# RWKV attention fused with an MLP: four chunks in pairs instead of six, other PSUM banks for the first pair, and weights loaded behind the second pair

## The chip, the cores and the metric

The kernel runs on one core of a Trainium2 chip. The core has five engines with an instruction stream each: TensorE (PE, matmuls and transposes into PSUM; PEld is its weight load), VectorE (DVE), ScalarE (ACT), GpSimd (POOL) and SyncE (SP, which issues transfers here). Sixteen DMA engines move data between HBM and the on-chip buffer SBUF. Each engine executes its own stream in order; semaphores make one wait for another. The metric is the device time of one execution in microseconds (us), lower is better.

## What is computed

Two steps in a row. The first is a recurrence with a decaying state per batch (4) and head (8), over 768 positions with 48 channels; the second is a two-layer MLP on the 3072 x 384 result.

```python
for t in range(S):                      # S = 768, B = 4, H = 8, D = 48
    cur = einsum('bhd,bhe->bhde', u[None] * k_t, v_t)
    y[:, :, t] = einsum('bhd,bhde->bhe', r_t, state + cur)
    state = w_t[..., None] * state + einsum('bhd,bhe->bhde', k_t, v_t)
x = y.transpose(0, 2, 1, 3).reshape(B * S, H * D)   # 3072 x 384
h = x @ w_in                            # 384 x 2048
g = maximum(0.01 * h, h)
out = g @ w_out                         # 2048 x 384
```

The decays w lie between 0.8 and 0.95. All inputs and the output are float32; the kernel multiplies in bfloat16 and accumulates in float32.

## The kernel before

The 3072 positions are 24 **chunks** of 128, six a batch. Inside a chunk the recurrence is made of matmuls: the logarithm of w (ScalarE) is summed along positions by a matmul with a triangular matrix of -1 (`cp`), its exponentials scale r and k (`rk`, products on VectorE), both are transposed (`rkT`, four 128 x 128 transposes for each of r and k, evacuated by VectorE from the bank `se` and by ScalarE from `so`), `scores` multiplies them, VectorE masks the result (`m`), and `intra` adds masked scores times v (`vb`) and scaled r times the incoming state (`sb`). The term with u is not in the matmuls: GpSimd multiplies r by u (`ru`) and by k, VectorE sums over channels (`dg`), GpSimd multiplies by v (`vs`), and VectorE adds that to the PSUM result (`y`). `outer` gives the new state. y is transposed into `xT`; then 4 groups of 12 up-projection matmuls a chunk (`hp`, leaky ReLU on ScalarE into `g`) and 4 quarters of 4 down-projection matmuls (`op`) make the output.

Some chunks come in **pairs**: 256 positions, of which every SBUF row holds two neighbours (j = 0, 1), so that a load has contiguous rows of 384 bytes instead of 192. A pair's matmuls work on two 64-row halves (`ab`, `par`, `q`).

The order of all engines is fixed when the program is built. `Plan` holds every step with an engine, an assumed duration, dependencies and a priority, and a list scheduler replays them; the instructions are then issued in the order found. A changed duration or priority in the source therefore changes orders, not work.

```python
    OACT = 14
    NCI = 3        # direct sums by matmul only for chunks below this
    NPE = 14       # from chunk 14 on, transposes go by DMA
    LEAD = 4       # logarithm of chunk n waits for the first up-projection of n - LEAD
    AHEAD = 5
    PAIRS = (0, 2, 4)
    WEIGHTS = [(2, 4.0)] * 2 + [(4, 24.0)] * 4 + [(6, 44.0)] * 2   # (chunk, priority)
    CASTS = 2
...
    hp_r = ring("hp", 2, [128, 512], F32, psum)
    op_r = ring("op", 2, [128, DM], F32, psum)
    cp_r = ring("cp", 1, [128, 512], F32, psum)
    yp_r = pp_r = ring("yp", 1, [128, 512], F32, psum)
    se_r = ring("se", 1, [128, NP, 128], F32, psum)
    so_r = ring("so", 1, [128, NP, 128], F32, psum)
```

Of a pair, the outer products, the state and the products with it:

```python
            for ab in range(2):
                q0 = 64 * ab
                ...                                      # sb: the incoming state, scaled on GpSimd
                pp = yp_r.take()
                def outer(pp=pp, q0=q0):
                    for p in range(NP):
                        for j in range(2):
                            nc.tensor.matmul(
                                pp.t[:, p * 2 * D : (p + 1) * 2 * D],
                                lhsT=rk[j].t[q0 : q0 + 64, 1, 2 * p : 2 * p + 2, :].rearrange("p h d -> p (h d)"),
                                rhs=vb[j].t[q0 : q0 + 64, 2 * p : 2 * p + 2, :].rearrange("p a d -> p (a d)"),
                                start=(j == 0), stop=(j == 1), skip_group_check=True)
                ...
            for jt in range(2):
                sc = [se_r.take(), so_r.take()]
                ...                                      # 32 score matmuls, mask
                def intra(m=m, yp=yp, jt=jt):
                    for ab in range(2):
                        if sbs[ab] is None: continue
                        for p in range(NP):
                            q = 64 * ab
                            nc.tensor.matmul(yp.t[q : q + 64, 2 * p * D : (2 * p + 2) * D],
                                lhsT=rkT[jt].t[:, p, q : q + 64], rhs=sbs[ab]..., ...)
                    ...                                  # 32 products of masked scores with v
```

Each of the eight weight loads (768 KB of w_in or w_out) is followed by a cast to bfloat16, half on VectorE and half on ScalarE. The row u is loaded by SyncE and spread over 128 partitions by a float32 matmul with a column of ones (`op` bank), then copied by ScalarE.

Of the kernel before, what the change touches and what calls it, by code (L numbers as in the profile page):

```python
# [15 lines left out]
class Plan:  # L16
# [5 lines left out]
    def __init__(self):  # L22
        self.eng, self.dur, self.fn, self.deps, self.pri, self.wire = [], [], [], [], [], []

    def add(self, eng, dur, fn, deps, pri, wire=None):

        i = len(self.eng)
        self.eng.append(eng)
        self.dur.append(dur)
        self.fn.append(fn)  # L30
        self.deps.append(sorted({d for d in deps if d is not None}))
        self.pri.append(pri)
        self.wire.append(wire)
        return i

    def order(self):
# [11 lines left out]
        dma_free = 0.0  # L48
        for i in range(n):
            if not left[i]:  # L50
                heapq.heappush(coming[self.eng[i]], (0.0, i))
# [3 lines left out]
        while events:  # L55
# [13 lines left out]
            free[e] = now + self.dur[i] * (1.8 if e == "PE" and now < 18 else 1)  # L69
            if self.wire[i] is None:  # L70
                done[i] = free[e] + self.LAT[e]
            else:
                dma_free = max(dma_free, free[e]) + self.wire[i]
                done[i] = dma_free + 1.6
            heapq.heappush(events, (free[e], e))
            for j in users[i]:
                left[j] -= 1
                ready_at[j] = max(ready_at[j], done[i])
# [37 lines left out]
def kernel(  # L116
# [26 lines left out]
    LEAD = 4  # L143
    AHEAD = 5

    PAIRS = (0, 2, 4)
    PWIRE, WIRE = 1.3, 1.15
    WEIGHTS = [(2, 4.0)] * 2 + [(4, 24.0)] * 4 + [(6, 44.0)] * 2
    CASTS = 2
# [43 lines left out]
    g_r = ring("g", 4, [128, NJ, max(blocks) * L], BF16)  # L193
# [3 lines left out]
    op_r = ring("op", 2, [128, DM], F32, psum)  # L197
    cp_r = ring("cp", 1, [128, 512], F32, psum)
    yp_r = pp_r = ring("yp", 1, [128, 512], F32, psum)
    se_r = ring("se", 1, [128, NP, 128], F32, psum)  # L200
    so_r = ring("so", 1, [128, NP, 128], F32, psum)

    with tc.manual_schedule():
# [51 lines left out]
        def step(eng, dur, fn, pri, reads=(), writes=(), deps=(), wire=None):  # L255
# [4 lines left out]
            i = plan.add(eng, dur, fn, d, pri, wire)  # L260
# [16 lines left out]
        def weight_steps(q, which, pri):  # L277
# [14 lines left out]
            ld = step("SP", 0.45, load, pri, writes=[st], wire=2.0)  # L292
# [44 lines left out]
        def product(rk, a, xn, e, P0, deps, n):  # L337
            return step(
                "DVE", 0.6 if n < 4 else 0.84 - 0.04 * a,
# [25 lines left out]
        def turn(rk, rkT, s_d, n, P0):  # L365

            if n >= NPE:
# [4 lines left out]
                    P0, reads=[rk], writes=[rkT], deps=s_d, wire=1.6)]  # L372
            made = []
            for a, eng in ((0, "DVE"), (1, "ACT")):
                tr = (se_r, so_r)[a].take()
                trv = tr.t[:].bitcast(BF16).rearrange("p g t -> p (g t)").rearrange("p (g t) -> p g t", t=128)
# [20 lines left out]
        def masked(m, sc, mask, s_sc, P0):  # L397
# [4 lines left out]
                        out=m.t[:, par], in0=sc[par].t[:],  # L402
# [14 lines left out]
        def state(sx, pp, sb, P0, deps):  # L417

            def f():
                i = pp.t[:, 0:DM].rearrange("p (g a d) -> p g a d", g=NP, a=2)  # L420
# [8 lines left out]
        def finish(yp, vs, s_y, s_vs, n, P0):  # L429
# [7 lines left out]
            if n >= NPE:  # L437
# [4 lines left out]
                    P0 + 1, reads=[y], deps=[s_ye], wire=0.65))  # L442
# [15 lines left out]
        def load_in(use, src, P0, i, n, wire, view):  # L458
            return step(
                "SP", 0.45, lambda: nc.sync.dma_start(out=view(use), in_=src), P0 + 0.1 * i,  # L460
                writes=[use], wire=wire, deps=[cums[n - AHEAD]] if n >= AHEAD else [])

        def spread_u():
            u_row = step(
                "SP", 0.45,
                lambda: nc.sync.dma_start(out=ur[:], in_=u.rearrange("h d -> (h d)").unsqueeze(0)),
                0.15, wire=0.05)
# [3 lines left out]
                lambda: nc.tensor.matmul(up.t[:], lhsT=onef[:], rhs=ur[:], start=True, stop=True),  # L471
                0, writes=[up], deps=[u_row])
            return step(
                "ACT", 0.5, lambda: nc.scalar.copy(out=ub[:], in_=up.t[:]), 3, reads=[up], deps=[s_ub])
# [6 lines left out]
        def pair(n):  # L481
# [89 lines left out]
            for j in range(2):  # L571
                s_T += turn(rk[j], rkT[j], s_d[j], n, P0)
# [3 lines left out]

            sbs, s_sbs = [], []
            for ab in range(2):
                q0 = 64 * ab
# [10 lines left out]
                pp = yp_r.take()  # L590

                def outer(pp=pp, q0=q0):
                    for p in range(NP):
                        for j in range(2):
                            nc.tensor.matmul(  # L595
                                pp.t[:, p * 2 * D : (p + 1) * 2 * D],
                                lhsT=rk[j].t[q0 : q0 + 64, 1, 2 * p : 2 * p + 2, :].rearrange("p h d -> p (h d)"),
                                rhs=vb[j].t[q0 : q0 + 64, 2 * p : 2 * p + 2, :].rearrange("p a d -> p (a d)"),
                                start=(j == 0), stop=(j == 1), skip_group_check=True)

                s_pp = step(
                    "PE", 0.35, outer, P0 + 1, reads=[*rk, *vb], writes=[pp],
                    deps=[s_d[0][1], s_d[1][1], *s_vb])
                sx = sx_r.take()
                prev = (sx, [state(sx, pp, sb, P0, [s_pp, *s_sb])])

            for jt in range(2):

                sc = [se_r.take(), so_r.take()]

                def scores(sc=sc, jt=jt):
                    for p in range(NP):
                        for js in range(2):
                            for q in (0, 64):
                                for par in range(2):
                                    q0 = 64 * par
                                    nc.tensor.matmul(
                                        sc[par].t[q : q + 64, p, 64 * js : 64 * js + 64],
# [4 lines left out]
                s_sc = step("PE", 0.6, scores, P0 + 1, reads=rkT, writes=sc, deps=s_T)  # L623
# [4 lines left out]
                def intra(m=m, yp=yp, jt=jt):  # L628
                    for ab in range(2):
                        if sbs[ab] is None:  # L630
                            continue
                        for p in range(NP):
# [18 lines left out]
                    "PE", 0.8, intra, P0 + 1, reads=[m, *vb, rkT[jt], *there], writes=[yp],  # L651
# [267 lines left out]
```

## Time and profile before

| | before |
|---|---|
| median of 3 runs | 196.09 us (195.69 to 196.6) |
| profiled span | 195.8 us |
| TensorE busy | 180.3 us (92%), 2680 matmuls |
| VectorE / ScalarE / GpSimd busy | 129.6 / 119.2 / 109.0 us |
| up-projection matmuls | 1152, 81.0 us busy |
| down-projection matmuls | 384, 77.0 us busy |
| moved by DMA | 33.92 MB, 173 GB/s on average |
| first up-projection matmul | 23.64 us |
| first / fourth / last output copied from PSUM | 48.45 / 66.37 / 192.40 us |

Busy time counts an engine from the start of an instruction to its modelled end. Matmuls are pipelined, so rows overlap: a group of 12 up-projection matmuls has a row of 0.83 us, but the next instruction of TensorE starts 0.67 us after it. Where work is added up below, the step from one row to the next is used. L12 means line 12 of the kernel's source, and a mark like SPq names the sequencer of an engine, here the time in which SyncE issues a transfer. "in" is the ring of input buffers, of w, k, r, v and weights alike.

### The profile page before, as it was taken

How to read it: one execution, taken by the hardware profiler on the slowest of the kernel's cores; microseconds unless marked ns; L12 is line 12 of the kernel's file. 1: busy time of each engine (PE TensorE's matmuls, PEld its weight loads, DVE VectorE, ACT ScalarE, POOL GpSimd, SP SyncE). 2: the span in 40 equal slices, each digit the busy share in tenths (PEclk: the TensorE clock that was granted, in tenths of full speed). 3: DMA queues.
4: the chain of work that ended last, by engine and by line, in shares of the span. 5: the costliest groups of instructions: out<-in, count | busy, mean ns of one | idle time of the engine just before them, and what ended most of it. 6: DMA issues, size and time to landing. Idle time of an engine off the chain costs nothing.

```text
span 195.8 us, 6457 instructions
## 1 busy us (share of the span) xinstructions
PE 180.3 (92%) x2680; PEld 141.3 (72%) x2680; DVE 129.6 (66%) x228; ACT 119.2 (61%) x256; POOL 109.0 (56%) x148
## 2 busy tenths in 40 slices
PE   0978399987999999999999999999999999999993
PEld 0355398784778878877877877877878778778771
DVE  2399955599698897976768568666869676541111
ACT  3655267577665876775878675757654656334430
POOL 7598905187997999889638647547534202100000
PEclk9999759999999999999999999999999999999999
DMA  6999998999998999786487696999942614711012
GB/s 160 300 327 293 380 313 243 244 255 190 186 258 174 217 223 209 157 172 136 112 159 162 146 197 146 204 177 179 201 94 64 142 49 116 97 60 55 11 41 82
DMA packets 109280, 33.92 MB, mean 173 GB/s; under 512 B 102593, under 2 KB 107714, under 8 KB 109250
## 3 DMA queue, kind: packets, MB, share of 16 engines
q1 hardware_dynamic: 109250, 33.50, 75.8%
q8 instruction: 21, 0.34, 0.7%
q14 instruction: 9, 0.07, 0.1%
HBM read 25.17 MB, written 4.72 MB: 153 GB/s over the span
## 4 chain that ended last, share of the span: by engine, by line
PE 83%; SPq 7%; DMA 4%; DVE 3%; issue 1%; ACT 1%; DVEq 0%
PE hp L808 33%; PE op L860 32%; SPq L460 5%; DMA in<-in_moe_w_in_dram 4%; PE se L738 3%; PE yp L772 2%; PE cp L679 2%; PE so L380 1%; PE yp L642 1%; PE yp L749 1%; DVE rk L340 1%; PE yp L767 1%; PE se L380 1%; SPq L282 1%; PE yp L448 1%
## 5 line engine op out<-in xcount | busy, mean ns | idle before, releaser
L842 ACT ACTIVATE g<-hp 128x512 bf16<-128x512 f32 x96 | 57.3, 597 | 42.5 <-PE hp L808 41.7
L808 PE MATMUL hp<-xT,w_in_b 128*128 128x128 bf16 x1152 | 81.0, 221 | 0.8 <-ACT xT L455 0.8
L860 PE MATMUL op<-w_out_b,g 128*128 128x384 bf16 x384 | 77.0, 326 | 0.9 <-DVE w_out_b L305 0.9
L808 PEld LDWEIGHTS <-w_in_b 128*128 128x128 bf16 x1152 | 70.7, 99 | 8.4 <-issue 1.1
L860 PEld LDWEIGHTS <-g 128*128 128x128 bf16 x384 | 33.1, 98 | 15.0 <-issue 1.0
L361 POOL TENSOR_TENSOR vs<-in,dg 128x384 f32<-128x384 f32 x24 | 21.2, 891 | 20.9 <-DVE y L434 12.9
L349 POOL TENSOR_TENSOR ru<-in,ub 128x384 f32<-128x384 f32 x24 | 26.2, 1100 | 7.7 <-DMA in<-in_r_dram 7.7
L353 POOL TENSOR_TENSOR ru<-ru,in 128x384 f32<-128x384 f32 x24 | 26.6, 1112 | 0.4
L410 POOL TENSOR_TENSOR sb<-s,a 128x384 bf16<-128x384 f32 x15 | 13.3, 887 | 20.9 <-DVE s L424 8.9
L340 DVE TENSOR_TENSOR rk<-in,er 128x384 bf16<-128x384 f32 x24 | 18.4, 768 | 9.2 <-DMA in<-in_r_dram 5.5
L434 DVE TENSOR_TENSOR y<-yp,vs 128x384 bf16<-128x384 f32 x24 | 13.3, 555 | 12.7 <-PE yp L772 9.2
L340 DVE TENSOR_TENSOR rk<-in,ek 128x384 bf16<-128x384 f32 x24 | 21.3, 887 | 0.1
L329 POOL CAST vb<-in 128x384 bf16<-128x384 f32 x24 | 14.5, 612 | 6.2 <-issue 4.3
L876 DVE COPY o<-op 128x384 f32<-128x384 f32 x10 | 5.6, 558 | 16.9 <-PE op L860 16.7
L401 DVE TENSOR_TENSOR m<-se,maskb 128x512 bf16<-128x512 f32 x18 | 12.4, 687 | 5.6 <-PE so L738 5.4
L357 DVE TENSOR_REDUCE dg<-ru 128x8 f32<-128x384 f32 x24 | 12.8, 543 | 3.9 <-POOL ru L353 3.8
L334 ACT ACTIVATE er<-cp 128x384 f32<-128x384 f32 x21 | 10.3, 489 | 7.1 <-DVE ci L704 5.5
L324 ACT ACTIVATE lw<-in 128x384 bf16<-128x384 f32 x24 | 12.3, 520 | 2.9 <-DMA in<-in_w_dram 2.9
L704 DVE TENSOR_TENSOR ci<-cp,lw 128x384 f32<-128x384 f32 x18 | 9.9, 551 | 4.6 <-ACT xT L455 2.3
L424 DVE TENSOR_TENSOR s<-yp,sb 128x384 f32<-128x384 f32 x16 | 8.8, 552 | 5.9 <-PE yp L595 3.5
L401 DVE TENSOR_TENSOR m<-so,maskb 128x512 bf16<-128x512 f32 x18 | 12.2, 679 | 0.0
L380 PEld LDWEIGHTS <-rk 128*128 128x128 bf16 x112 | 8.6, 108 | 3.7 <-DVE rk L340 1.9
(93 smaller groups left out, 213.4 us busy)
## 6 DMA issues: line engine op xcount, KB each, us to landing
out_dram<-o SPq DMA_DIRECT2D x24, 192.0 KB, 2.2
in<-in_w_dram SPq DMA_DIRECT2D x18, 192.0 KB, 3.6
in<-in_k_dram SPq DMA_DIRECT2D x18, 192.0 KB, 3.7
in<-in_r_dram SPq DMA_DIRECT2D x18, 192.0 KB, 3.9
in<-in_v_dram SPq DMA_DIRECT2D x18, 192.0 KB, 3.7
in<-in_moe_w_in_dram SPq DMA_DIRECT2D x4, 768.0 KB, 7.6
in<-in_moe_w_out_dram SPq DMA_DIRECT2D x4, 768.0 KB, 9.6
in<-in_w_dram SPq DMA_DIRECT2D x3, 384.0 KB, 8.2
```

Source lines behind the costliest of these rows:

```text
L329: "POOL", 0.57, lambda: nc.gpsimd.tensor_copy(out=vb.t[:], in_=vn.t),
L340: lambda: nc.vector.tensor_tensor(out=rk.t[:, a, :, 0:D], in0=xn.t, in1=e.t[:], op=ALU.mult),
L349: lambda: nc.gpsimd.tensor_tensor(out=ru.t[:], in0=rn.t, in1=ubv, op=ALU.mult),
L353: lambda: nc.gpsimd.tensor_tensor(out=ru.t[:], in0=ru.t[:], in1=kn.t, op=ALU.mult),
L357: lambda: nc.vector.tensor_reduce(out=dg.t[:], in_=ru.t[:], axis=AX.X, op=ALU.add),
L361: lambda: nc.gpsimd.tensor_tensor(out=vs.t[:], in0=vn.t, in1=dg.t[:].unsqueeze(2).to_broadcast([128, H, D]), op=ALU.mult),
L401: lambda par=par: nc.vector.tensor_tensor(out=m.t[:, par], in0=sc[par].t[:], in1=mask.unsqueeze(1).to_broadcast([128, NP, 128]), op=ALU.mult),
L410: lambda: nc.gpsimd.tensor_tensor(out=sb.t[:].rearrange("p g a d -> p (g a) d"), in0=s_in.t[:].rearrange("p g a d -> p (g a) d"), in1=a_ap ...
L434: lambda: nc.vector.tensor_tensor(out=y.t[:], in0=hd(yp.t[:, 0:DM]), in1=vs.t[:], op=ALU.add),
L808: nc.tensor.matmul(hp.t[:, a * N : (a + 1) * N], lhsT=w_in_b[:, t, (j + a) * 128 : (j + a + 1) * 128], rhs=xT[:, t, c0 : c0 + N], start=(a ...
L842: lambda hp=hp, g=g, j=j, J=J, N=N: nc.scalar.activation(out=g.t[:, j : j + J, 0:N], in_=hp.t[:, 0 : J * N].rearrange("p (a n) -> p a n", ...
L860: nc.tensor.matmul(op.t[:], lhsT=g.t[:, j, off : off + 128], rhs=w_out_b[:, j, :], start=(j == 0), stop=(j == NJ - 1))
```

## The change

It has these parts:

- Only chunks 0 to 3 are paired; chunks 4 and 5 become singles.
- In the first pair, chunk 1's transposes and scores go to the two `hp` banks, and both outer products to the two `op` banks, which lie idle then, instead of waiting for `se`, `so` and `yp`. In the second pair the outer products go to `se` and `so`.
- A pair's outer products of both 64-row halves are issued alternately, each half into its own bank; the state products of `intra` alternate between the two halves as well.
- u's row is issued from ScalarE's queue, and its matmul is given the first priority.
- One weight load stands between the w, k and the r, v loads of the second pair, and the other seven follow behind that pair; their casts get a lower priority.
- `LEAD` goes from 4 to 8, the ring `g` from 4 buffers to 3, and the scheduler's assumptions change (a limit of rows in flight for transfers, a longer slow phase of TensorE, no latency inside one engine).

It is meant to let the first two pairs through before the weights, to shorten their chain, and to spare TensorE work.

```diff
-    LEAD = 4
+    LEAD = 8
-    PAIRS = (0, 2, 4)
-    PWIRE, WIRE = 1.3, 1.15
-    WEIGHTS = [(2, 4.0)] * 2 + [(4, 24.0)] * 4 + [(6, 44.0)] * 2
-    CASTS = 2
+    PAIRS = (0, 2)
+    PWIRE, WIRE = 1.45, 1.15
+    WEIGHTS = [(2, 20.15)] + [(4, 24.0)] * 7
+    CASTS = 3
...
-    g_r = ring("g", 4, [128, NJ, max(blocks) * L], BF16)
+    g_r = ring("g", 3, [128, NJ, max(blocks) * L], BF16)
...
-            free[e] = now + self.dur[i] * (1.8 if e == "PE" and now < 18 else 1)
+            free[e] = now + self.dur[i] * (1.8 if e == "PE" and now < 26 else 1)
...
+                flying = [x for x in flying if x[0] > free[e]]
+                while sum(x[1] for x in flying) + self.rows[i] > 3300:
+                    free[e] = max(free[e], flying.pop(0)[0])
...
             u_row = step(
-                "SP", 0.45,
-                lambda: nc.sync.dma_start(out=ur[:], in_=u.rearrange("h d -> (h d)").unsqueeze(0)),
-                0.15, wire=0.05)
+                "ACT", 0.5,
+                lambda: nc.scalar.dma_start(out=ur[:], in_=u.rearrange("h d -> (h d)").unsqueeze(0)),
+                -1, wire=0.05)
...
-                s_T += turn(rk[j], rkT[j], s_d[j], n, P0)
+                s_T += turn(rk[j], rkT[j], s_d[j], n, P0, (hp_r, hp_r) if j and n == 0 else (se_r, so_r))
...
+            pps = [op_r.take(), op_r.take()] if n == 0 else [se_r.take(), so_r.take()]
+            def outer():
+                for p in range(NP):
+                    for j in range(2):
+                        for ab in range(1 if last else 2):
+                            q0 = 64 * ab
+                            nc.tensor.matmul(
+                                gt(pps[ab].t)[:, p, 0 : 2 * D],
+                                lhsT=rk[j].t[q0 : q0 + 64, 1, 2 * p : 2 * p + 2, :].rearrange("p h d -> p (h d)"),
+                                rhs=vb[j].t[q0 : q0 + 64, 2 * p : 2 * p + 2, :].rearrange("p a d -> p (a d)"),
+                                start=(j == 0), stop=(j == 1), skip_group_check=True)
...
-                sc = [se_r.take(), so_r.take()]
+                sc = [hp_r.take(), hp_r.take()] if jt and n == 0 else [se_r.take(), so_r.take()]
...
-                    for ab in range(2):
-                        if sbs[ab] is None:
-                            continue
-                        for p in range(NP):
+                    for p in range(NP):
+                        for ab in range(2):
+                            if sbs[ab] is None:
+                                continue
```

## The prediction

> **What bounds the kernel now.** I read the page's table of slices first, then the chain that ended last, then the chain, the waits and a table of stretches for the first 50 us only.
>
> The row of TensorE and the chain's shares by engine, from the page:
>
> ```profile
> PE   0978399987999999999999999999999999999993
> PE 83%; SPq 7%; DMA 4%; DVE 3%; issue 1%; ACT 1%; DVEq 0%
> ```
>
> A slice is 4.9 us. From the eleventh slice on TensorE is full until the last. So the kernel is TensorE's work, plus what is lost in the first 50 us, plus a tail. The reader is to see the hole in the fifth slice (19.6 to 24.5 us, 3 tenths), the empty first slice, and that 7% and 4% of the chain are SyncE's queue and a transfer.
>
> The table of stretches (busy us of each engine, granted clock, share of the DMA engines, GB/s):
>
> ```profile
> 10.00:15.00 5.00, 3.69 (x61) 2.77 (x59) 4.52 (x8) 2.84 (x6) 5.00 (x6) 1.00 1.16 319
> 20.00:25.00 5.00, 2.44 (x19) 1.94 (x19) 4.67 (x7) 1.99 (x3) 4.58 (x6) 0.70 1.06 379
> ```
>
> The DMA engines are full (a share of 1 and more) while VectorE, the third busy number, is full too: 4.5 and 4.7 of 5 us. TensorE is the idle one. The chain up to 50 us, in order of time, says what it waited for:
>
> ```profile
> 9.40 3.27 SPq L460
> 12.72 1.49 SPq L460
> 14.21 0.04 issue
> 14.26 7.98 DMA in<-in_moe_w_in_dram
> 22.23 0.02 issue
> 22.26 0.02 ACT w_in_b L307
> 22.28 0.83 issue
> 23.11 0.49 ACT xT L455
> 23.60 0.04 issue
> 23.64 1.44 PE hp L808 x12
> ```
>
> Loads of pair two, then of the third quarter of w_in, then its cast, then xT: the first up-projection starts at 23.64. But TensorE's own list of waits shows a second cause:
>
> ```profile
> PE yp L448 <- DVE y L434: 3.2, 1, 3.2
> ```
>
> Chunk 0's product ended at about 18.7, yet VectorE formed its y only at 21.60, because its fixed order had four products for pair two (17.46 to 21.7, one waiting for r) in front of it. Earlier it sat on weight casts (10.78, 12.86) in front of pair one's evacuations (11.81 and 13.91). The weights are in the way of pair one and pair two, on the wire and on VectorE.
>
> **What the Trainium skill says.** "TensorE: Matmul & The Clock Gate", Part 1, has TensorE at half clock until about 3.4 us of dense work. The trace agrees: a group of 12 up matmuls takes 1.44 us at 23.64, 0.98 at 28.56 and 0.67 later; sparse work from 5 to 19 us did not warm it. "TensorEngine Tiling (Array Packing)", Restrictions and Gotchas, lets different row tiles run at once, but not into the same bank. The old outer products put both 64-row halves into one bank, one after the other: 0.82 us for 8 cold, 0.44 warm. The new ones alternate halves and banks. "DMA: Bandwidth & Descriptors", Issuing engines are not separate DMA queues, says another issuing engine saves only issue time; here that is the 0.47 us that the u row held SyncE. Its Specifications ask for 512 B for full rate: in fine stretches of the trace the pair loads (384 B rows) move 262 GB/s and the weights (1.5 and 2 KB) 380.
>
> **The work on TensorE.** In full stretches an up group takes 0.67 us and a down quarter 0.65 in the chain. 24 chunks x 4 of each: 64.3 + 62.4 = 126.7 us, unchanged.
> Attention, warm, from chain pieces and starts of rows. A pair: running sums 0.62 (0.43 + 0.19), direct sums 4 x 0.17 = 0.68 (first two pairs only), transposes 4 x 0.22, outer 2 x 0.44, scores 2 x 0.32, state and inner products 2 x (0.30 + 0.55), y transposes 2 x 0.17: 5.74, or 5.06 for pair three. A single: 0.27 + 0.44 + 0.33 + 0.17 + 0.16 + 0.20 + 0.17 = about 1.75, and 1.14 from chunk 14, where DMA transposes.
> Before: 2 x 5.74 + 5.06 + 8 x 1.75 + 10 x 1.14 = 41.9; total 168.6. The last matmul ends at 192.4, so about 24 us are lost. By the same prices 6.1 us of work is done when the first up starts at 23.64 (17.5 lost); 12 ups, 8 downs and 7.0 of attention, 20.3 in all, are done from there to 49.7 (5.7 lost: cold clock about 2.4, the rest waits on VectorE and the last weights); about 0.8 is lost later.
>
> **The change part by part.**
> 1. Pair three becomes two singles: 5.06 to 3.5, **-1.6 us** of TensorE. VectorE's sum is about even. Its loads become 192 B rows, which move 210 GB/s at 50 to 80 us, so 1 to 2 us more wire, behind the weights.
> 2. Side by side: outer products 0.88 to 0.44 and state products 0.60 to 0.30 a pair, on two pairs: 2 x 0.74 = **-1.5 us**. I take the full factor of two. Some falls in waits, but cold prices double it.
> 3. Idle banks for pair one: chunk 1's transposes go to the hp banks, the outer products to both op banks, its scores to hp. They no longer wait for se and so to be evacuated (before: the last transposes at 12.27, scores at 14.36).
> 4. u: 0.47 us less on SyncE. On ScalarE it follows the table load (0.80 to 2.08), so it lands at about 4.6, and its matmul (1.64 cold) now stands first on TensorE. The running sums shift from 4.85 to about 6.2. The direct sums stay at about 7.5, since u stood in front of them before. A wash.
> 5. Weights behind pair two. At 262 and 380 GB/s and with the lag of landing that the trace shows (1 us early, 2.8 later): pair two's w at about 10, w_in first quarter 13.8, r 15.6, v 17.6, the other quarters 19.7, 22.3, 24.6, w_out 26.7, 28.8, 30.9, 32.9. Before, w came at 14.37, r at 17.46, and the last of w_out was cast at 44.7.
> 6. The lead goes from 4 to 8 chunks and the g ring from 4 to 3. Chunks 4 to 7 no longer wait for an up-projection before their logarithm, and chunk 3's g waits for chunk 0's down-projection. No instruction is added; I price it at nothing, because the seams between chunks cost only 0.8 us in all after 49.7.
>
> Following the new order of each engine with the old durations: products of pair one end at 10.6 on VectorE as before, evacuations at 11.5 and 12.0 (before 14.3), scores 12.2 to 13.6, masks to 16.3, chunk 0's product 15.9, y 16.9, xT 18.2 (before 23.6). Chunk 1's product fills to 19.5 and the **first up starts at 20.1**. By then 6.2 us of work is done: 13.9 lost instead of 17.5.
> From there w_out sets the pace: the last quarter is cast at about 33.8, and the order has the fourth down of chunk 0 in front of chunk 2's product. By about 38, 8 ups, 8 downs and both pairs are done, 14.5 us of work in 17.9: 3.4 lost, instead of 5.7. Chunk 4's inputs land at about 37, its xT at 47.5, when TensorE has just run out of chunks 2 and 3: I add 0.7 and allow 1.5 after 38.
> Sum: work 126.7 + 38.8 = 165.5; lost 13.9 + 3.4 + 1.5 = 18.8; last matmul 184.3. The tail from the last matmul to the end stays 3.4, and the median lies 0.3 above the profiled span: **188.0 us**, 8.1 less: 3.1 of work, 5.0 of waits.
>
> **The rivals.**
> *The wait only moves.* In-order TensorE stands at w_out or at chunk 4's input. For it: weights now come last, w_out and chunk 4 are within 1 to 2 us of need, the singles' rows are slow, and the DMA engines are full to 80 us in the old trace. Against it: chunks 1 to 3 hold 16 us of up and down work meanwhile. If 3 to 4 us are lost there, 191 to 192.
> *VectorE or GpSimd becomes the bound of the start.* VectorE is at 90% from 10 to 25 us already, and the 8 casts still sit between its steps. If it runs 2 us behind my walk, 190.
> *Warm earlier.* Denser work could warm TensorE at 20 instead of 24 us: 186.
> *The start doesn't matter.* With the bound on TensorE from 50 us on, only the 3.1 of work would come off: 193. Against it: work left at 50 us counts one to one, as only 0.8 us are lost after that.
>
> **Range and chances.** Most rivals cost, the warm clock gains: 184.5 to 192.0. Faster by over 2% means under 192.2, missed only if nearly all of the start's gain is lost: 0.84. Within 2%: 0.13. Slower: 0.03, if the looser lead (8 chunks) or the smaller g ring starves the middle.
>
> **What would show it.** First up at about 20 and xT of chunk 0 near 18; evacuations at 12; the 16 outer products within 0.9 us cold; the last w_out cast near 34; four chunks' outputs by about 54 (before 66.4); chunk 4's xT by 48; intervals between outputs of 6 to 7 us after. It is wrong if TensorE has idle slices between 25 and 50 us, if the first up stays past 22, or if w_out lands after 36.

## The result, and the profile after

The change takes the kernel from 196.34 us (195.69 to 197.66) to **190.33 us** (190.19 to 190.66), medians of four runs each on one chip: a ratio of 0.9688, 95% interval 0.9635 to 0.9741. The profiled span goes from 195.8 to 189.0 us, but the profiled execution of the kernel before took 197.47 us, 1.1 more than its median, so the spans overstate the gain. The forecast was 188.0 in a range of 184.5 to 192.0: the gain is 6.0 us where 8.1 were expected.

The row of TensorE in the table of slices and the chain's shares by engine, from the page of the changed kernel:

```profile
PE   3688899999999999999999999999999999999992
PE 76%; DMA 10%; SPq 9%; DVE 1%; issue 1%; ACT 1%; ACTq 0%
```

A slice is 4.7 us here. The hole in the fifth slice is gone, and TensorE is full from the sixth slice (before: the eleventh) to the end. The shares of the chain by engine have moved towards transfers (10% and 9%), though TensorE does not wait more for them: the chain is followed back from the end through whatever was last, and it now reaches the weight loads without passing a late evacuation.

The same stretches as before, with the busy us of TensorE, its weight loads, VectorE, ScalarE and GpSimd, then the granted clock, the DMA share and GB/s:

```profile
10.00:15.00 5.00, 4.17 (x103) 3.09 (x102) 4.65 (x9) 2.97 (x6) 4.97 (x7) 1.00 1.17 312
20.00:25.00 5.00, 4.28 (x43) 3.99 (x40) 4.73 (x8) 3.65 (x6) 2.90 (x3) 1.00 1.06 380
```

From 20 to 25 us TensorE works 4.28 us instead of 2.44, with VectorE and the DMA engines as full as before (4.73 us, a share of 1.06), and the granted clock is 1.00 instead of 0.70. The stretches from 26 to 38 and 38 to 50 us have 11.89 and 12.00 us of TensorE out of 12; before they had 12.00 and 10.01. From 26 us to the last matmul it is idle for 0.3 us in all.

The chain of the start, in order of time:

```profile
10.75 3.16 SPq L290
...
15.59 1.96 SPq L295
17.60 13.10 DMA in<-in_moe_w_out_dram
...
30.71 0.57 DVE w_out_b L313
...
31.33 0.81 PE op L873 x4
```

L290 and L295 are the issues of w_in's and w_out's loads. Before, the chain went through pair two's loads, the third quarter of w_in and xT to the first up-projection at 23.64. Now the attention of pairs one and two is off it, up to a quarter of w_out that is in the queue from 17.60 to 30.69, is cast, and releases four down-projection matmuls at 31.33. This is hardly a wait: the up-projections in front of them end at 31.25, so TensorE stands still for 0.08 us. Up-projections and attention fill the time.

The wait that pointed to chunk 0's late y (3.2 us before) is down to

```profile
PE yp L458 <- DVE y L444: 0.7, 1, 0.7
```

### The profile page after: what moved, and what is told of

It is laid out like the page before. It is cut to its first block, busy times and chain, and to the rows that moved or that the text cites. A ratio compares the mean times of both kernels' runs of the same rounds, so it can differ in the third digit from the quotient of the medians.

```text
span 189.0 us, 6273 instructions
## 1 busy us (share of the span) xinstructions
PE 177.9 (94%) x2572; PEld 140.3 (74%) x2572; DVE 128.1 (68%) x228; ACT 117.6 (62%) x258; POOL 108.3 (57%) x148
## 4 chain that ended last, share of the span: by engine, by line
PE 76%; DMA 10%; SPq 9%; DVE 1%; issue 1%; ACT 1%; ACTq 0%
PE op L873 31%; PE hp L821 30%; DMA in<-in_moe_w_out_dram 7%; SPq L470 4%; PE se L750 3%; SPq L290 3%; DMA in<-in_w_dram 3%; PE yp L785 2%; PE yp L761 2%; PE cp L691 2%; PE yp L780 1%; SPq L295 1%; PE so L391 1%; PE yp L458 1%; PE se L391 1%
## 5 line engine op out<-in xcount | busy, mean ns | idle before, releaser
L357 POOL TENSOR_TENSOR ru<-in,ub 128x384 f32<-128x384 f32 x24 | 25.5, 1063 | 13.2 <-DMA in<-in_r_dram 13.2
L361 POOL TENSOR_TENSOR ru<-ru,in 128x384 f32<-128x384 f32 x24 | 25.5, 1064 | 0.9
L348 DVE TENSOR_TENSOR rk<-in,er 128x384 bf16<-128x384 f32 x24 | 19.7, 821 | 8.4 <-DMA in<-in_r_dram 5.4
L421 POOL TENSOR_TENSOR sb<-s,a 128x384 bf16<-128x384 f32 x17 | 15.8, 930 | 14.5 <-DVE s L434 10.6
L412 DVE TENSOR_TENSOR m<-se,maskb 128x512 bf16<-128x512 f32 x20 | 13.7, 686 | 6.7 <-PE so L750 6.6
L337 POOL CAST vb<-in 128x384 bf16<-128x384 f32 x24 | 15.3, 640 | 1.2 <-DMA in<-in_v_dram 1.2
L412 DVE TENSOR_TENSOR m<-so,maskb 128x512 bf16<-128x512 f32 x20 | 13.6, 680 | 0.0
L342 ACT ACTIVATE er<-cp 128x384 f32<-128x384 f32 x22 | 10.9, 496 | 2.5 <-DVE ci L716 2.2
L716 DVE TENSOR_TENSOR ci<-cp,lw 128x384 f32<-128x384 f32 x20 | 11.0, 548 | 1.6 <-ACT g L855 1.6
L342 ACT ACTIVATE ek<-ci 128x384 f32<-128x384 f32 x20 | 10.6, 528 | 0.0
## 6 DMA issues: line engine op xcount, KB each, us to landing
out_dram<-o SPq DMA_DIRECT2D x24, 192.0 KB, 2.9
in<-in_w_dram SPq DMA_DIRECT2D x20, 192.0 KB, 3.9
in<-in_k_dram SPq DMA_DIRECT2D x20, 192.0 KB, 3.8
in<-in_r_dram SPq DMA_DIRECT2D x20, 192.0 KB, 3.9
in<-in_v_dram SPq DMA_DIRECT2D x20, 192.0 KB, 3.7
```

Of the source, the lines that this page charges most:

```text
L337: "POOL", 0.57, lambda: nc.gpsimd.tensor_copy(out=vb.t[:], in_=vn.t),
L342: "ACT", 0.5, lambda: nc.scalar.activation(out=out.t[:], in_=i, func=AF.Exp, scale=scale),
L348: lambda: nc.vector.tensor_tensor(out=rk.t[:, a, :, 0:D], in0=xn.t, in1=e.t[:], op=ALU.mult),
L357: lambda: nc.gpsimd.tensor_tensor(out=ru.t[:], in0=rn.t, in1=ubv, op=ALU.mult),
L361: lambda: nc.gpsimd.tensor_tensor(out=ru.t[:], in0=ru.t[:], in1=kn.t, op=ALU.mult),
L412: lambda par=par: nc.vector.tensor_tensor(out=m.t[:, par], in0=gt(sc[par].t), in1=mask.unsqueeze(1).to_broadcast([128, NP, 128]), op=ALU.m ...
```

## The experiments

The theory was that the start alone sets the gain, by the parts priced in the prediction, which add up. The rivals were that one part carries nearly all of it and the rest is ornament, or that something not priced (the scheduler's assumptions, a warmer TensorE) carries it. Each kernel is the changed one with one part undone unless it says otherwise. Columns: median; ratio to the kernel before on the same chip, with its interval; and what the undoing costs, worked out as (ratio minus 0.9688) times 196.3 us. The changed kernel's own ratio is uncertain by 1.0 us in that unit and the other rows' by 0.5 to 0.9, so costs under about 1.3 us are no costs. One of the four runs of x_wold (195.61) is slow; it is in the median but not in the ratio.

| kernel | undone or altered | median us | ratio, 95% interval | cost us |
|---|---|---|---|---|
| b_weights | before, with the new weight places only | 195.26 | 0.9930 [0.9902, 0.9959] | (gains 1.4) |
| x_wold | weight places back | 192.46 | 0.9773 [0.9735, 0.9811] | 1.7 |
| x_pair3 | third pair back | 193.08 | 0.9811 [0.9780, 0.9841] | 2.4 |
| x_banks | pair one in `se`, `so` alone | 194.31 | 0.9871 [0.9835, 0.9908] | 3.6 |
| x_usp | u back on SyncE | 192.96 | 0.9789 [0.9761, 0.9818] | 2.0 |
| x_outer_serial | outer products half after half | 190.65 | 0.9682 [0.9655, 0.9709] | -0.1 |
| x_intra_serial | state products half after half | 190.19 | 0.9658 [0.9629, 0.9687] | -0.6 |
| x_sched | all three assumptions of the scheduler back | 199.14 | 1.0110 [1.0081, 1.0140] | 8.3 |
| x_noflying | only the limit of rows in flight back | 200.79 | 1.0183 [1.0136, 1.0231] | 9.7 |
| x_18 | only the short slow phase back | 190.74 | 0.9679 [0.9638, 0.9720] | -0.2 |
| x_warmfill | idle matmuls added early | 191.04 | 0.9696 [0.9657, 0.9735] | 0.2 |
| x_npe12 | DMA transposes from chunk 12 | 190.20 | 0.9683 [0.9644, 0.9723] | -0.1 |

### The weights' places, alone and undone

```diff
-    WEIGHTS = [(2, 20.15)] + [(4, 24.0)] * 7
-    CASTS = 3
+    WEIGHTS = [(2, 4.0)] * 2 + [(4, 24.0)] * 4 + [(6, 44.0)] * 2      # x_wold; b_weights is the reverse, in the kernel before
+    CASTS = 2
```

> The changed kernel with the old places of the weight loads (two in front of pair two, the rest with chunks 4 and 6) and the old priority of casts; all else as changed. Theory of the prediction (weights in the way of the pairs): first up-projection back from 20.4 to 22.5 to 23.5 us, last w_out cast back from 32.9 to 40 or later, TensorE idle again at 20 to 25 and 40 to 50 us; 193.5 to 195. Rival (the start does not matter, only TensorE's work came off): within 0.5 us of the changed kernel, 190 to 191.

> The kernel before with the new places and priorities of the weight loads and nothing else. Theory: pair two's w, k, r land some 4 us earlier and no cast stands before pair one's evacuations, but pair one still waits for se, so and yp, and pair three for its loads behind all weights: first up at 21.5 to 22.5, 193 to 195. Rival (the order of weights is the whole gain of the start): first up at 20.5, 191.5 to 192.5. Second rival (pair three's inputs now come too late and the order gives nothing by itself): 196 or more.

In b_weights the first up-projection starts at 23.54, as before and not at 21.5 to 22.5: the weights are out of the way, but the chain to chunk 0's xT is as long as ever, and TensorE's longest wait after 6 us is still that for chunk 0's y (2.2 us). What it gains, it gains later: TensorE is full from 38 to 50 us (12.00 against 10.01), and the last half quarter of w_out is cast at 36.6 and not at 44.7. It loses 1.4 us again at 140 to 150, in one wait for a DMA transpose. In x_wold xT of chunk 0 comes at 19.05 and the last half quarter of w_out is cast at 37.8 and not at 32.9, but TensorE is not idle from 40 to 50 us as expected (12.00 of 12 from 38 to 50). The loss lies from 26 to 38 us:

```profile
26.00:38.00 12.00, 10.68 (x205) 8.20 (x205) 7.43 (x14) 8.11 (x16) 6.08 (x8) 0.86 0.98 254
```

1.3 us of TensorE idle and a granted clock of 0.86. The idle time is one wait,

```profile
PE se L594 <- DVE rkT L399: 1.3, 1, 1.3
```

for an evacuation of pair two (27.64) that VectorE does behind a cast of w_out (26.52): the weights are in the way of pair two on VectorE, as the prediction had it. The places are worth about 1.5 us from either side. They are not what most of the gain is made of.

### The third pair

```diff
-    PAIRS = (0, 2)
+    PAIRS = (0, 2, 4)
```

> The changed kernel with chunks 4 and 5 as a pair again. Theory: a pair costs TensorE 5.06 less the side-by-side saving of outer products 0.44, so 4.6 us against 3.5 for two singles: +1.1 us, 191.4. Rival (the wire counts: 384 B rows move 262 GB/s, 192 B rows 210, and chunk 4 came only just in time): as fast or up to 1 us faster than the changed kernel, 189.5 to 190.3. If the pair's longer chain makes TensorE wait for chunk 4: 193 and more, with an idle slice at 45 to 55 us.

The start is the same to 50 us. Then chunk 4's xT, which as a single came at 49.65, comes at 54.30, and TensorE, which has 9.83 us of work in this stretch in the changed kernel, runs out of it:

```profile
50.00:60.00 10.00, 9.46 (x209) 7.25 (x207) 9.49 (x16) 6.00 (x15) 7.19 (x8) 1.00 0.96 207
```

0.54 us idle here (0.4 more than in the changed kernel) and 0.3 later, beside the 1.1 us of matmuls expected, make 1.8 of the 2.4 us that it costs; the rest lies within the uncertainty.

### The banks of the first pair

```diff
-                s_T += turn(..., (hp_r, hp_r) if j and n == 0 else (se_r, so_r))
-            pps = [op_r.take(), op_r.take()] if n == 0 else [se_r.take(), so_r.take()]
-                sc = [hp_r.take(), hp_r.take()] if jt and n == 0 else [se_r.take(), so_r.take()]
+                s_T += turn(..., (se_r, so_r))
+            pps = [se_r.take(), so_r.take()]
+                sc = [se_r.take(), so_r.take()]
```

> The changed kernel with pair one in the banks se and so throughout (transposes, scores and outer products, as in pair two), no idle banks. Theory: chunk 1's transposes wait for the evacuation of chunk 0's and its scores for the mask of chunk 0's: pair one ends 1.5 to 2.5 us later, first up at 22 to 23, 191.5 to 192.5. Rival (hidden: the up-projections wait for w_in's quarters at 20.3, 22.3 and 24.4 anyway): first up later but 190 to 190.8.

The largest part of the start, at 3.6 us. The first up-projection starts at 27.73, four us later than in the kernel before, and chunk 0's xT starts at 25.41. This does not go back to the kernel before: there the outer products had the bank `yp`, here transposes, outer products and scores all share two banks, so 3.6 us is not what the idle banks gained over the kernel before. TensorE's waits in the start:

```profile
PE yp L458 <- DVE y L444: 2.3, 1, 2.3
...
PE so L391 <- DVE rk L348: 2.2, 2, 2.0
PE yp L654 <- DVE m L412: 1.5, 2, 1.2
```

Leaving the first-pair chain in two banks puts the evacuations between its steps: the outer products start at 13.75 instead of 12.04, and the first bank is free for scores at 15.17, where the changed kernel starts them at 12.80. The rest of the delay is order: pair two's sums go ahead of the scores (15.90), VectorE forms products for pair two (17.07, 17.54) in front of pair one's first mask (18.81 instead of 13.48), and two more (20.93, 21.93) in front of chunk 0's y (23.21). TensorE then has 10.97 us of work in the first 20 us instead of 13.63, and 3.11 of 6 from 20 to 26 instead of 5.28. That the idle banks shorten pair one's chain is shown, by about 2.4 us up to the scores; how much of the 3.6 us they are worth without the new order is not, and my estimate of the size was too low.

### u's row

```diff
-                "ACT", 0.5, lambda: nc.scalar.dma_start(out=ur[:], ...), -1, wire=0.05)
+                "SP", 0.45, lambda: nc.sync.dma_start(out=ur[:], ...), 0.15, wire=0.05)
...                                   # its matmul -1 -> 0, the copy 0.05 -> 3
```

> The changed kernel with u's row on SyncE's queue and the old priorities of its matmul and copy. Prediction: a wash, since u's landing at 4.6 would push the running sums to 6.2. The trace of the changed kernel shows u on ScalarE at 0.83, in front of the end of the table load, and its matmul in the otherwise idle 2.4 to 4.0 us: so undoing it should move the direct sums from 6.0 to 7.5 and cost 0.3 to 1.2 us (190.6 to 191.5) if pair one's products wait for the exponentials, and nothing if they wait for r, which lands at 7.6.

The first row is the changed kernel, the other two are x_usp:

```profile
2.37 0.97 PE L481 MATMUL op<-ur,onef 1*128 1x384 f32 x1 [2.37 <-DMA ur<-in_u_dram]
```

```profile
6.13 1.64 PE L481 MATMUL op<-ur,onef 1*128 1x384 f32 x2
7.71 0.82 PE L521 MATMUL hp<-lw,pev 128*128 128x384 bf16 x2
```

The prediction let u land at about 4.6, after ScalarE's table load. But ScalarE's queue issued it at 0.83, beside the table load (0.80 to 2.08), and its matmul starts at 2.37, while TensorE has nothing else to do before 5.05. So the 1.6 us of slow float32 matmul leave the path, and the direct sums start at 5.99 instead of 7.54; in x_usp they stand at 7.71 again.

That does not bring pair one's transposes forward. With u there, GpSimd multiplies r by u from 7.62 on, and the next product of VectorE takes 1.35 us beside it instead of 0.55. The changed kernel, then x_usp, where GpSimd starts at 8.38:

```profile
8.05 1.35 DVE L348 TENSOR_TENSOR rk<-in,ek 128x384 bf16<-128x384 f32 x1
9.33 1.34 DVE L348 TENSOR_TENSOR rk<-in,er 128x384 bf16<-128x384 f32 x1
```

```profile
8.13 0.55 DVE L348 TENSOR_TENSOR rk<-in,ek 128x384 bf16<-128x384 f32 x1
9.09 0.87 DVE L348 TENSOR_TENSOR rk<-in,er 128x384 bf16<-128x384 f32 x1 [0.40 <-ACT er L342]
14.13 1.01 DVE L313 CAST w_in_b<-in 128x768 bf16<-128x768 f32 x1 [1.02 <-DMA in<-in_moe_w_in_dram]
15.07 0.67 DVE L412 TENSOR_TENSOR m<-se,pmask 128x512 bf16<-128x512 f32 x1
```

Pair one's products end at 11.45 in the changed kernel and at 10.73 in x_usp. What x_usp loses, it loses after that, by its order: pair two's sums go ahead of pair one's scores (13.03 instead of 12.80), VectorE waits for a quarter of w_in to cast it in front of the first mask (15.07 instead of 13.48), and ScalarE waits for the next quarter (20.22) in front of xT, which comes at 20.96 instead of 18.12. The first up-projection starts at 24.49 instead of 20.43. So the 2.0 us are what undoing u costs together with the order that it makes; that the earlier u saves time by itself is not shown.

### Side by side

```diff
-            for p ...: for j ...: for ab ...:      # x_outer_serial, the outer products
+            for ab ...: for p ...: for j ...:
-            for p ...: for ab ...:                 # x_intra_serial, the state products
+            for ab ...: for p ...:
```

> The changed kernel with the outer products of the two 64-row halves one half after the other (same banks, same order of all steps). Prediction's term: 2 pairs x 0.44 us warm, the first pair cold (0.8): 16 products take 0.88 warm and 1.6 cold instead of 0.44 and 0.8; 0.5 to 1.2 us slower, 190.8 to 191.5. Rival (hidden in waits for weights): under 0.3 us.

> The changed kernel with the state products of a pair in the old order (one half's four, then the other half's). Prediction's term: 0.30 us a pair lost again on the two pairs, 0.5 us slower with the cold one, and 8 state products take 0.30 instead of 0.15 us. Rival, read from the trace of the changed kernel (8 products in 0.29 us, as before): no packing took place, no difference at all in the row and under 0.2 us in time.

Neither can be seen in the time, since the half us that each was priced at on both pairs lies below what these comparisons resolve. They can be seen in the rows. The 16 outer products of pair one, cold, in the changed kernel and in x_outer_serial:

```profile
12.04 0.82 PE L594 MATMUL op<-vb,rk 64*128 64x96 bf16 x16
```

```profile
11.98 1.13 PE L594 MATMUL op<-vb,rk 64*128 64x96 bf16 x16
```

The kernel before took 0.82 for eight. Warm, in pair two, the 16 take from 28.64 to the next instruction at 29.09, 0.45 us, as the prediction had it (0.44). One half after the other, but still in two banks, takes 0.63, not 0.88: the second half begins before the first is through. The starts show it: from 29.06 to 29.18 products of both halves take turns. So part of the factor of two comes without alternating. How much of the 0.25 us between 0.88 and 0.63 the second bank gives is not shown, because 0.88 is two groups, each with its own change to the next instruction (0.14 us from the start of the last product in the changed kernel).

The state products behave otherwise. In the chain, the changed kernel and x_intra_serial:

```profile
34.59 0.29 PE yp L646 x8
38.24 0.29 PE yp L646 x8
```

```profile
34.62 0.30 PE yp L646 x8
38.28 0.30 PE yp L646 x8
```

Eight products take 0.29 to 0.30 us in either order, as in the kernel before (0.30). Nothing runs side by side here. They use all 128 rows and split the columns, and both halves write one bank. The Trainium skill, "TensorE: Matmul & The Clock Gate", Part 3, The mechanism, says that a weight load overlaps running matmuls only where their row groups differ. That alone does not decide it: a group of 12 up-projections uses all rows too, and its 12 weight loads of 0.10 us each go by in 0.67 us. Whether the rows or the shared bank keep the state products apart stays open.

### The scheduler's assumptions

```diff
-                while sum(x[1] for x in flying) + self.rows[i] > 3300:      # x_noflying, x_sched
+                while sum(x[1] for x in flying) + self.rows[i] > 10**9:
-            ... (1.8 if e == "PE" and now < 26 else 1)                      # x_18, x_sched
+            ... (1.8 if e == "PE" and now < 18 else 1)
-                ready_at[j] = max(ready_at[j], free[e] if same else done[i])   # x_sched
+                ready_at[j] = max(ready_at[j], done[i])
```

> The changed kernel planned with the old assumptions of the scheduler (slow TensorE to 18 us only, no limit of rows in flight, latency inside an engine). Theory (parts and not assumptions make the gain): within 0.7 us, 189.8 to 191. Rival (the order is the gain): 192 or more. Its order has fourth down quarters bunched behind the last w_out cast, so TensorE would wait at about 33 us.

> The changed kernel planned without the limit of rows in flight alone; the other two assumptions stay new. With all three old the start was equal (first up at 20.7) and TensorE lost 6 us at 120 to 135 us, waiting for masks behind DMA transposes that came later than planned. Theory (the limit makes the plan wait for a full queue, so it places work behind transposes realistically): 196 to 199, with the idle time at the first DMA transposes. Rival (it is one of the other two, or chance of the order): 189.5 to 191.5.

> The changed kernel planned with TensorE slow to 18 instead of 26 us and nothing else. Theory (this shifts only the early order): at most 1 us, 190 to 191.3, all of it before 50 us. Rival (any shift of the early order reshuffles the whole plan, and the hand-over to DMA transposes can go wrong again): 193 or more, with idle time after 100 us.

The biggest surprise. Without the limit of rows in flight the change is slower than the kernel before (1.0183), though its start is the same (first up-projection at 20.45). The row of TensorE in x_noflying's page:

```profile
PE   3688899999999999999999999429999999999993
```

The hole is at 125 to 135 us, in the middle. The stretches of x_noflying, then those of the changed kernel:

```profile
120.00:130.00 10.00, 7.19 (x95) 4.71 (x93) 9.49 (x16) 4.17 (x13) 8.30 (x9) 0.97 1.25 184
130.00:140.00 10.00, 6.11 (x66) 5.20 (x65) 6.53 (x12) 3.33 (x8) 6.91 (x9) 0.51 0.67 142
```

```profile
120.00:130.00 10.00, 10.00 (x141) 7.92 (x140) 7.62 (x14) 6.21 (x15) 7.68 (x8) 1.00 0.86 167
130.00:140.00 10.00, 10.00 (x158) 8.11 (x158) 8.51 (x16) 6.61 (x16) 4.12 (x5) 1.00 0.85 173
```

6.7 us of idle TensorE, and a clock of 0.51 from 130 to 140 us. The kernel before has no such hole: its TensorE is busy for 142.00 of the 142 us from 50 to 192. So the limit adds nothing that the kernel before lacked; it keeps the other parts from losing time here. The rows of chunk 14, the first whose transposes go by DMA, tell how it comes about: its attention, its xT, and the first up-projection from it, in x_noflying,

```profile
119.60 0.36 PE L785 MATMUL yp<-vb,m 128*128 128x48 bf16 x8
121.17 0.57 SPq L470 DMA_DIRECT2D in<-in_w_dram  x1
...
123.39 1.03 SPq L470 DMA_DIRECT2D in<-in_v_dram  x1
124.52 1.49 SPq L450 DMA_TRANSPOSE xT<-y  x1
132.70 0.22 PE L785 MATMUL yp<-vb,m 128*128 128x48 bf16 x1 [2.48 <-DVE m L412]
135.07 4.04 PE L821 MATMUL hp<-xT,w_in_b 128*128 128x128 bf16 x36
```

and the first two of these in the changed kernel:

```profile
115.83 0.36 PE L785 MATMUL yp<-vb,m 128*128 128x48 bf16 x8
117.87 1.21 SPq L450 DMA_TRANSPOSE xT<-y  x1
```

The limit tells the scheduler that SyncE stops issuing while many rows are outstanding. Without it, the scheduler lets loads pass at a fixed 0.45 us of SyncE each, and orders all four loads of a coming chunk in front of the transpose of a y that is ready (VectorE starts it at 120.00 and needs 0.56 us, the transpose is issued at 124.52; in the changed kernel at 116.23 and 117.87). By 124 us TensorE has done all 14 x 48 up and 14 x 16 down matmuls of chunks 0 to 13 (672 and 224 in the trace) and has only attention of chunks 15 to 17 in front of the next up-projection, which waits for VectorE (9.52 of 10 us busy from 124 to 134) step by step. What TensorE's list of waits names is VectorE's masks and y, not a transpose:

```profile
PE yp L785 <- DVE m L412: 4.4, 4, 2.5
PE yp L761 <- DVE y L444: 1.7, 2, 1.0
```

In the changed kernel chunk 15's attention is done by 124 us, one chunk more, and 674 and 220 MLP matmuls. So the hole is attention that comes too late in TensorE's order for the MLP work that should cover it. That the order was fitted to transposes earlier than the real ones is argued from the rule of the scheduler, not read from its plan. The 36 up-projections at 135.07 take 4.0 us, 1.32 a group of 12 instead of 0.67.

x_sched has the same hole (6.58 of 10 us busy from 120 to 130), and x_18, with the slow phase alone put back, is as fast as the changed kernel. So of the three assumptions the limit is the one that carries; the third, no latency inside one engine, was not put back alone, but with all three old the cost is no larger (8.3 us). Whether it would help the kernel before, with `LEAD` at 4 and three pairs, was not tried.

### A warmer start, and a later use of the transposes

```diff
+            if seen in FILL: warm(FILL[seen])       # x_warmfill: 42 matmuls of a constant into an unused bank, in the first 13 us
-    NPE = 14                                         # x_npe12
+    NPE = 12
```

> The changed kernel with 42 matmuls of no use (128 x 128, into the idle bank yp) in TensorE's gaps before 12 us, so that its clock may be full from about 8 us on. Prediction's rival (warm earlier): first up near 19 us in 0.83 instead of 1.49 us, up to 2 us less, 188.3 to 189.5. Theory from the runs so far (the kernel with serial state products happened to be warm at 20.0 us and was no faster, 190.2): the quarters of w_in and w_out set the pace from 20 to 33 us, so 190 to 190.7. If the filler gets in the way of pair one: 191.

> The changed kernel with DMA transposes from chunk 12 instead of 14, an attempt at a faster one. TensorE is full from 26 us to the end, so two chunks fewer of transposes on it (8 x 0.055 for r and k and 0.17 for y, 0.61 us a chunk) should take off 1.2 us: 189.1, if the DMA engines have room (share 0.9 to 0.96 at 60 to 140 us, loads waiting for buffers there). Rival, from the two plans that went wrong at the hand-over: the transposes land later than planned and TensorE stands behind them: 191 or more, idle time at 85 to 110 us.

x_warmfill does warm TensorE: the first up-projection starts at 19.05 and a group has a row of 0.83 us, where the changed kernel has 1.49 at 20.43; chunk 0's xT comes at 17.05. It gains nothing, because from 20 to 26 us TensorE is now idle instead of slow:

```profile
20.00:26.00 6.00, 2.51 (x39) 2.26 (x40) 5.74 (x9) 4.61 (x8) 2.87 (x4) 1.00 1.06 380
```

x_intra_serial turned out warm at 20.01 by itself (0.83 a group) and has 3.50 us of 6. In x_warmfill 2.7 us of the idle time are one wait:

```profile
22.58 0.34 PE L466 MATMUL yp<-ident,y 128*128 128x128 bf16 x3 [2.69 <-DVE y L452]
```

VectorE forms this y, chunk 1's, at 21.98, and in the changed kernel at 22.04: its order has in front a cast of a quarter of w_in, which starts as the quarter lands (20.12 and 20.27), and a product for pair two. The DMA engines move 374 to 380 GB/s in all three. So here the arrival of w_in and VectorE's order set the pace, and not TensorE's clock.

x_npe12 was meant to beat both kernels by taking the transposes of chunks 12 and 13 off TensorE. Its six runs spread from 188.78 to 191.51 us. In the profiled one, at 191.47, the span is 189.8 us and the saved matmuls come back as idle time from 140 to 160 us (0.34 and 1.10 us), one wait for a chunk's logarithm among it:

```profile
PE cp L691 <- ACT lw L332: 1.1, 1, 1.1
```

No kernel tried here is faster than the changed one by more than the uncertainty.

## Why the prediction was right, and where it was off

| step | predicted | measured |
|---|---|---|
| VectorE's evacuations of pair one end | 11.5, 12.0 | 11.78, 12.12 |
| pair one's scores start | 12.2 | 12.80 |
| 16 outer products, cold | within 0.9 | 0.82 |
| chunk 0's xT; first up-projection | 18.2; 20.1 | 18.12; 20.43 |
| last cast of w_out starts | about 33.8 | 32.88 |
| chunk 4's xT | 47.5 | 49.65 |
| fourth output | 54 | 57.99 |
| last matmul ends | 184.3 | 185.3 |
| last matmul to end of span | 3.4 | 3.7 |
| median over span | 0.3 | 1.3 |

The first five rows are the mechanism, and they held: the walk of the new order of each engine with durations from the old trace came within 0.4 us of the first up-projection, and within a us of the weights. The kernel is still bound by TensorE's work plus what the start loses, and the three last rows make up the 2.3 us between 188.0 and 190.33: 1.0 + 0.3 + 1.0.

**The step from span to median was wrong.** The 0.3 us set the median of the kernel before, 196.09, against the span of another execution, one of 197.47 us. Every run here takes 1.7 to 1.9 us more than its own span (197.47 over 195.8, 190.66 over 189.0). With 1.7 the same sum gives 189.4, which leaves 0.9 of the 2.3 us to the kernel.

**The state products failed** (part 2). They were to fall from 0.60 to 0.30 us a pair on two pairs, 0.6 us in all; each of a pair's two groups of eight still takes 0.29 to 0.30. The outer products, the other term of the same part, held (0.45 for 0.44). The work is then 126.7 + 39.4 = 166.1, and with a last matmul at 185.3 the loss is 19.2, against the 18.8 of the sum.

**u was walked wrongly** (part 4). The step that failed is its landing at 4.6 us behind the table load; the matmul had it at 2.37. Two errors cancelled, which was luck: the direct sums came 1.5 us earlier than walked, but VectorE's products, now beside GpSimd's, took 1.35 us where the walk had the old durations, and the last of pair one ended at about 11.5 instead of 10.6; xT came out as forecast. Undone, with the order that this makes, u costs 2.0; by itself it may still be the wash that was forecast.

**The scheduler's assumptions were not in the sum at all.** The lead and the smaller ring `g`, priced at nothing, were not tried alone, nor were the changed durations that the scheduler assumes. The limit of rows in flight is worth 9.7 us to the changed kernel, more than the whole gain, though at a place where the kernel before lost nothing. The prediction came right without it because the order as built already has the limit's effect in it: the walk took that order for the start, and assumed for the rest that almost nothing is lost, which only the limit made true.

**The parts do not add up.** The costs of undoing the banks, the third pair, u, the weights and the limit are 3.6 + 2.4 + 2.0 + 1.7 + 9.7 = 19.4 us, for a change that gains 6.0. Each undoing makes the scheduler find another order. The theory that the priced parts add up falls. That one part alone carries the gain does not fit either, since five undoings cost 1.7 to 9.7 us each; of the parts only the weights' places were tried alone, and they give 1.4.

**The rivals.** "The wait only moves": in part. Chunk 4's xT came 2 us later than walked, but TensorE was full of other work (12.00 of 12 us from 38 to 50), so that nothing was lost; the fourth output at 58 is order, not idle time. "VectorE or GpSimd becomes the bound": not for long. VectorE ended pair one's products 0.9 us behind the walk and had caught up at xT, and after 26 us TensorE is idle for 0.3 us. "Warm earlier": refuted by x_warmfill and by x_intra_serial, which were warm at 19 to 20 us and not faster. "The start doesn't matter": refuted by the time, which fell by 6.0 us, of which only 2.5 by the prediction's prices (1.6 of the third pair, 0.9 of the outer products) are work. The waits gave 3.5, where 5.0 were forecast.

## What to carry to other kernels

When a scheduler fixes the order of all engines, read a change in the order it builds, engine by engine, and test its parts by undoing each: a part's worth depends on the order found with the others. What such a scheduler assumes of the issue queue can decide as much as the parts: here one line of it was worth 9.7 us, in a stretch where the kernel before had lost nothing. An early result on one engine can also slow another, as u did. And if products are put side by side, look at their rows for it: a factor of two that the order of the loop suggests may not be there.

## What the runs showed of the hardware

- 64-row products of two halves into two banks overlap even when issued half after half: 0.63 us for 16, against 0.45 alternated and 0.88 in one bank (twice 0.44 for 8). Products of all 128 rows on two column halves of one bank gain nothing from alternating: 0.29 to 0.30 for 8 in either order.
- VectorE's products of two SBUF operands take 1.34 to 1.35 us beside GpSimd's products of ru (changed kernel, 8.05 and 9.33), 0.85 beside its cast of v (changed kernel, 10.60), and 0.55 where GpSimd is idle as they start (x_usp, 8.13).
- ScalarE's queue issues a transfer at 0.83 us while ScalarE loads its table from 0.80 to 2.08.
- The moment at which TensorE becomes warm differs between kernels that differ by one loop's order: an up group takes 0.83 us at 20.0 in one and 1.49 at 20.4 in the other. The granted clock of both records is 1.00 there; it does not show this phase. With one trace of each kernel, the loop cannot be told from a change from run to run.
- With 4.1 us of TensorE's work in the 10 us from 124 to 134 and no single wait over 2.5 us, x_noflying's granted clock fell: 0.77 in that stretch, 0.51 from 130 to 140. x_warmfill, with 2.5 us of work from 20 to 26 and a wait of 2.7, kept 1.00.
